# Read-back weight conversions, another order of the PSUM pools and pinned first sevens in an attention + two-MLP kernel

## The chip, the cores and the metric

The kernel runs on one core of a Trainium2 chip. The metric is the device time of one execution in microseconds (us). A core has five engines with queues of their own: TensorE (PE; its weight loads are listed as PEld), VectorE (DVE), ScalarE (ACT), GpSimd (POOL) and SyncE (SP, which here only issues transfers). SBUF is the working memory of 128 partitions, PSUM the eight banks into which PE writes. Every engine takes its own instructions in the order in which they stand in its queue; between engines they wait on semaphores.

## The reference

```python
scores = scale * (q @ k.T); bias = -(cum[:, None] - cum[None, :])      # cum = cumsum(relu(s))
attn = softmax(where(causal, -1e9, scores + minimum(bias, 0)))          # 2 batches, 8 heads, 576 x 576, head size 64
x = (attn @ v) as 1152 tokens x 512
h = x @ w_in; x = maximum(0.01 * h, h) @ w_out                          # 512 -> 2048 -> 512, weights float64
out = sum over 4 experts e of p[:, e] * (maximum(x @ w1[e], 0) @ w2[e]) # 512 -> 1024 -> 512
```

Everything is kept at about fp32 accuracy: a matrix operand is split into a high part (`hi`, rounded to fp32r) and a low part (`lo`, the rest), and a product is three matmuls, hi·hi, lo·hi and hi·lo.

## The kernel before

**Three stages.** In the first, attention runs as 16 *units* (a batch, a pair of heads, the first 256 or the last 320 queries; units 0 to 7 have the first queries, 8 to 15 the last), and the first MLP for the 512 tokens of the first queries (`phases[0]`, functions `opening`, `up1`, `down1`) is woven into it: a matmul group of the MLP between the steps of attention keeps PE busy. When attention ends, what is left of that MLP runs alone: a down block of 48 matmuls, an up piece of 24 and a last down block of 48. In the second stage the first MLP runs for the other 640 tokens, in the third the experts, both with products saved by sums of quarters of the operands (`paired_up`): each weight piece becomes a *seven*, seven sums of quarters of it, hi and lo.

**Attention.** An *item* is one tile of 128 queries of one head. Its steps stand in a pipeline: `scores` (PE writes `ps_sc`, DVE makes `z` and its minimum `mn`), one item later `exps` (ACT on `z`), then `transposes` (PE into `ps_pt`, ACT copies to `pv`), `values` (PE into `ps_o`; at a unit's end DVE normalizes into `xo`), and `finish` (PE transposes `xo` into `ps_x`, ACT copies it to `x`). For units 8 to 15 the keys and queries are split by `split_keys`, one unit ahead: ACT casts `qs`, `ks` and `kd` (`kd` holds the keys once more, beside two rows of `cum` that a transfer brings), POOL makes the low parts of `qs` and `ks`.

**Weights.** `w_in` and `w_out` come as float64. A generator, `supply`, makes them fp32 in 16 *conversions*, each a row of small steps (`converted`): ACT takes the absolute value of the upper words into a `raw` tile, DVE does four operations on it (two `TENSOR_SCALAR`, two `SCALAR_TENSOR_TENSOR`), then `split_w` casts it into a `w` tile (ACT: hi; POOL: lo), and ACT issues a transfer that stores the fp32 values in `w_f32` in HBM, from where the second stage reads them. There are 3 `raw` buffers and 4 `w` buffers (`wpool`). A `w` tile comes free when PE has used it; the split of the fifth conversion and of all later ones so waits for PE, and since ACT takes its queue in order, everything behind the cast waits too. Conversion steps are laid between the attention steps by fixed rules (the loops at lines 707 to 737) and the last ones between the steps of the rest of the MLP (line 746).

**Order.** Up to line 753 every instruction is kept in the order in which it is written (`fixed`, class `InOrder`). Only `fetch`, which loads the weights of the later stages, sets `fixed` to False for itself, and so a scheduler places the loads and sevens of the second stage where it estimates them to fit; from line 753 on the scheduler orders everything.

**PSUM.** While attention runs, the eight banks belong to `ps_mm` (3 banks, MLP), `ps_s` (2, scores), `ps_t` (2, transposes) and `ps_o` (1), in that order. After attention the four pools are closed and `ps_all` takes all eight (line 744). Its tiles go round from the first bank, so its first tile lies where `ps_mm` lay, and may be written only when the tile that was there has been read.

In the profile all instructions go through the recording helper at line 43, so they are told apart by tile names: `raw`, `w` (the sevens' tile is also shown as `w`), `sums` (POOL's sums of quarters), `kd`, `ks`, `qs`, `z`, `pv`, `ht` and `ps_u` (hidden layer), `ps_d` and `y` (down product), `t` (paired tokens), `w_f` (the stored weights).

Of the kernel before, what the change touches and what calls it, by code (L numbers as in the profile page):

```python
# [15 lines left out]
PSUM = bass.MemoryType.PSUM  # L16
# [3 lines left out]
def attention_moe_moe2(ctx: ExitStack, tc: tile.TileContext, q, k, v, s, w_in, w_out, probs, w1, w2, out):  # L20
# [10 lines left out]
    fixed = True  # L31
# [29 lines left out]
    RAW = 3  # L61

# [53 lines left out]
    def converted(n):  # L116

        _, shape, unit = stream[n][:3]
        raw = rawp.tile([P, 1024], F32, tag="raw", name="raw")
        raws.append(raw)  # L120
# [12 lines left out]
        ready.append(split_w(raw, shape, False))  # L133
        nc.scalar.dma_start(w_f32[unit], raw)
        yield

    def supply():

        for n in range(2 * DFF // P // 2):
            yield from converted(n)  # L140
            if len(r64s) < 2 * DFF // P // 2:
                fetch64(len(r64s))
# [10 lines left out]
    def seven(raw):  # L153

        r = raw.rearrange("p (k f) -> p k f", k=KD)
# [5 lines left out]
        nc.gpsimd.tensor_tensor(sums[:, 3], a12, sums[:, 1], ALU.subtract)  # L161
        w = w7pool.tile([P, 2, 7, 2, P], F32R, tag="w7", name="w7", bufs=2)
# [4 lines left out]
        return w  # L167
# [31 lines left out]
    stream, r64s, raws, ready = [], [], [], []  # L199

    def fetch(n):

        nonlocal fixed
        if w7pool is None or len(ready) < 2 * DFF // P // 2:
            return
        was, fixed = fixed, False
        while len(raws) < min(n, len(stream)):
            raws.append(load_w(*stream[len(raws)][:3]))
        while len(ready) < len(raws):
            ready.append(split_w(raws[len(ready)], stream[len(ready)][1], stream[len(ready)][4]))  # L210
        fixed = was

    used, w7pool = 0, None

    def next_w(k):

        nonlocal used
        used += k
        fetch(used + look)
        return ready[used - k : used]  # L220
# [40 lines left out]
    def opening(h):  # L261

        w = next_w(1) + next_w(1)
# [167 lines left out]
    banks = ctx.enter_context(ExitStack())  # L431
    ap = attn.enter_context(tc.tile_pool(name="attn", bufs=2, side="right"))
    ps_mm = banks.enter_context(tc.tile_pool(name="ps_mm", bufs=3, space=PSUM))
    ps_s = banks.enter_context(tc.tile_pool(name="ps_s", bufs=2, space=PSUM))
    ps_t = banks.enter_context(tc.tile_pool(name="ps_t", bufs=2, space=PSUM))
    ps_o = banks.enter_context(tc.tile_pool(name="ps_o", bufs=1, space=PSUM))

# [108 lines left out]
    def split_keys(n):  # L546

        qr, kr = k_raw.pop(n)
# [9 lines left out]
        nc.scalar.copy(kd[:D], kr)  # L558
# [137 lines left out]
    with ExitStack() as phase:  # L696
# [3 lines left out]
        side, units_of_w, opened = attention(), supply(), 0  # L700
        nothing = ps_mm.tile([P, 512], F32, tag="mm", name="nothing")
        with tc.tile_pool(name="early", bufs=1) as early:
# [4 lines left out]
            for at_ in range(3 * 64):  # L707
                i = next(side)
# [10 lines left out]
                if at_ % 3 == 2:  # L719
                    if i in (1, 5):  # L720
                        fetch64(i // 4)
                    if i >= 9 and (i < 19 or i % 2):
                        next(units_of_w)
# [3 lines left out]
        for at_, i in enumerate(side):  # L727
# [5 lines left out]
            else:  # L733
                given += 1.2
# [75 lines left out]
```

## Time and profile before

| what | value |
|---|---|
| runs | 748.47, 749.66, 751.17 us; median 749.66 us |
| the profiled execution | 749.58 us, of which the trace spans 747.8 us |
| PE | busy 718.2 us, 96% of the span, 4388 matmuls |
| DVE, ACT, POOL | busy 418.8, 330.0 and 323.2 us |
| mean granted TensorE clock | 0.990 |
| HBM | 52.58 MB read, 10.82 MB written |

The profile is one execution. The page of slices shows attention in the first 15 or so of 40 slices; from there PE is full to the end. PE's idle time lies before 260 us almost alone. The granted clock is 1.0 (2.4 GHz) but for a few stretches of 0.5 (1.2 GHz): near 54 us, and twice between 220 and 255 us. A time in brackets in a timeline row, `[1.22 <-ACT pv L43]`, is how long the engine sat idle before that row and who ended it.

### The profile page before, as it was taken

The numbers are of one execution on the slowest core, as the hardware profiler recorded it, in microseconds if no ns is written. First come the engines' busy times: TensorE is split into PE (matmuls) and PEld (weight loads), VectorE is DVE, ScalarE is ACT, GpSimd is POOL, SyncE is SP. The second block draws the span as 40 slices with busy tenths as digits, with TensorE's granted clock in tenths as the row PEclk, the third lists the DMA queues.
The fourth block names the chain that finished last, engine by engine and source line by source line (L and its number), as shares of the span: only waits on it lengthen the run. The fifth ranks groups of instructions, "written<-read, shape, count | busy, mean of one in ns | idle before, by whom it ended". The sixth has DMA issues, their size and how long they took to land.

```text
span 747.8 us, 11394 instructions
## 1 busy us (share of the span) xinstructions
PE 718.2 (96%) x4388; PEld 651.2 (87%) x4388; DVE 418.8 (56%) x850; ACT 330.0 (44%) x643; POOL 323.2 (43%) x250
## 2 busy tenths in 40 slices
PE   9889989999998899999999999999999999999998
PEld 8778778888776699999988988989889899898996
DVE  3765686587558545763684443544435445354452
ACT  4677787875653365553351231322314223142220
POOL 4144334443229568894346270542705526143200
PEclk9998999999999999999999999999999999999999
DMA  6794465632432223221011110201102012020002
GB/s 163 203 290 116 135 188 166 179 98 85 167 143 85 58 85 109 88 86 57 30 57 56 57 57 2 85 29 56 57 1 82 33 57 57 0 67 20 1 29 98
DMA packets 39450, 64.14 MB, mean 86 GB/s; under 512 B 3844, under 2 KB 22820, under 8 KB 39396
## 3 DMA queue, kind: packets, MB, share of 16 engines
q1 hardware_dynamic: 30692, 38.26, 17.9%
q10 hardware_dynamic: 8704, 25.17, 9.9%
q8 instruction: 34, 0.56, 0.3%
q14 instruction: 20, 0.16, 0.1%
HBM read 52.58 MB, written 10.82 MB: 85 GB/s over the span
## 4 chain that ended last, share of the span: by engine, by line
PE 83%; DVE 5%; ACT 5%; POOL 3%; issue 3%; ACTq 0%; POOLq 0%; DVEq 0%
PE ps_d L43 38%; PE ps_u L43 32%; PE ps_o L43 5%; PE ps_sc L43 4%; PE ps_pt L43 3%; DVE raw L43 2%; PE nothing L43 2%; POOL w L43 2%; POOL sums L43 1%; ACT w L43 1%; ACT z L43 1%; DVE z L43 1%; ACT raw L43 1%; ACT pv L43 1%; DVE t L43 1%
## 5 line engine op out<-in xcount | busy, mean ns | idle before, releaser
L43 POOL TENSOR_TENSOR w<-raw,w 128x1024 fp32r<-128x1024 f32 (+2 forms) x88 | 147.7, 1694 | 320.7 <-ACT w L43 307.4
L43 PE MATMUL ps_u<-t,w 128*128 128x320 f32 (+1 forms) x1680 | 237.3, 299 | 2.2 <-DVE t L43 1.1
L43 PEld LDWEIGHTS ps_u<-t,w 128*128 128x128 f32 x1680 | 233.2, 189 | 6.3 <-ACT w L43 1.5
L43 PE MATMUL ps_d<-w,ht 128*128 128x512 f32 x864 | 203.3, 391 | 0.0
L43 PEld LDWEIGHTS ps_d<-w,ht 128*128 128x128 f32 x864 | 160.2, 188 | 31.9
L43 ACT ACTIVATE ht<-ps_u 128x320 fp32r<-128x320 f32 (+2 forms) x176 | 74.3, 433 | 158.0 <-DVE ps_u L43 132.0
L43 PE MATMUL ps_d<-ht,w 128*128 128x320 f32 (+1 forms) x576 | 113.5, 346 | 7.8 <-DVE y L43 4.3
L43 ACT CAST w<-raw 128x1024 fp32r<-128x1024 f32 (+2 forms) x88 | 64.0, 758 | 95.8 <-PE ps_d L43 82.0
L43 PEld LDWEIGHTS ps_d<-ht,w 128*128 128x128 f32 x576 | 92.9, 192 | 15.1 <-issue 4.7
L43 DVE SCALAR_TENSOR_TENSOR oacc<-ps_d,pn,oacc 128x512 f32<-128x512 f32 x63 | 47.3, 751 | 104.3 <-PE ps_d L43 104.3
L43 PEld LDWEIGHTS ps_o<-vs,pv 128*128 128x128 f32 x480 | 64.1, 193 | 9.3 <-issue 3.6
L43 DVE TENSOR_TENSOR ps_u<-ps_u,tmp 128x320 f32<-128x320 f32 (+1 forms) x120 | 56.4, 471 | 27.7 <-PE ps_u L43 26.3
L43 DVE SCALAR_TENSOR_TENSOR ht<-ps_u,ht 128x320 fp32r<-128x320 f32 (+1 forms) x128 | 56.3, 452 | 23.3 <-ACT ht L43 22.0
L43 PE MATMUL ps_o<-vs,pv 128*128 128x65 f32 x480 | 63.2, 268 | 3.4 <-DVE xo L43 2.3
L43 POOL TENSOR_TENSOR w<-sums,w 128x1024 fp32r<-128x1024 f32 x24 | 57.9, 2412 | 8.4 <-ACT w L43 8.4
L43 DVE TENSOR_TENSOR tmp<-ps_u,tmp 128x320 f32<-128x320 f32 (+1 forms) x80 | 36.9, 464 | 42.5 <-PE ps_u L43 37.3
L43 PE MATMUL ps_u<-x,w 128*128 128x512 f32 x192 | 58.2, 418 | 0.0
L43 ACT ACTIVATE z<-z,mn 128x256 f32<-128x256 f32 (+4 forms) x80 | 48.6, 607 | 18.6 <-DVE mn L43 16.2
L43 DVE CUSTOM_DVE_ANT_0 z<-ps_sc,mask 128x256 f32<-128x256 f32 (+4 forms) x80 | 40.9, 512 | 26.9 <-PE ps_sc L43 12.4
L43 PE MATMUL ps_pt<-ident,z 128*128 128x128 f32 x240 | 40.9, 279 | 7.5 <-ACT pv L43 7.4
L43 DVE TENSOR_TENSOR ht<-ps_u,ht 128x320 fp32r<-128x320 f32 (+1 forms) x48 | 26.5, 555 | 36.9 <-ACT ps_u L43 36.9
L43 DVE SCALAR_TENSOR_TENSOR raw<-r,raw 128x1024 uint32<-128x1024 uint32 x32 | 45.7, 1429 | 0.2
(72 smaller groups left out, 645.6 us busy)
## 6 DMA issues: line engine op xcount, KB each, us to landing
raw<-in_moe_w_dram SPq DMA_DIRECT2D x32, 512.0 KB, 3.6
r<-in_moe_w_in_dram ACTq DMA_DIRECT2D x8, 1024.0 KB, 7.6
w_f<-raw ACTq DMA_DIRECT2D x16, 512.0 KB, 3.0
r<-in_moe_w_out_dram ACTq DMA_DIRECT2D x8, 1024.0 KB, 5.0
raw<-w_f SPq DMA_DIRECT2D x16, 512.0 KB, 3.4
qr<-in_q_dram SPq DMA_DIRECT2D x16, 160.0 KB, 3.1
kr<-in_k_dram SPq DMA_DIRECT2D x8, 288.0 KB, 7.4
vs<-in_v_dram SPq DMA_DIRECT2D x8, 256.0 KB, 4.2
```

Of the source, the lines that this page charges most:

```text
L43: ins = call(*args, **kw)
```

## The change

- **Store first, split only where a tile is free.** `converted` now issues the store and then splits at once only if unit n's `w` buffer was used by pieces that the MLP has already gone past (`n < retired + WB`, `retired` is set in `next_w`). Otherwise the `raw` tile is given up, and a second generator, `late_splits`, later reads the fp32 values back from HBM (SP's queue) and splits them.
- **Rhythm.** No conversion steps at items 19 to 28; 2.0 steps per item instead of 1.2 at items up to 49, then 1.25. All 16 conversions end before attention does.
- **First sevens pinned.** The two sevens that the second stage starts with are no longer placed by the scheduler; `first_sevens` lays their steps between the MLP's last steps, in written order.
- **PSUM.** `ps_mm` is opened last, so the first five tiles of `ps_all` lie where `ps_s`, `ps_t` and `ps_o` were.
- **`kd` cast on POOL** instead of ACT (8 casts).

```diff
     def converted(n):
@@
-        ready.append(split_w(raw, shape, False))
         nc.scalar.dma_start(w_f32[unit], raw)
+        if n == len(ready) and n < retired + WB:
+            ready.append(split_w(raw, shape, False))
         yield
+    def late_splits():
+
+        while len(ready) < CONVERTED:
+            n = len(ready)
+            if n < min(retired + WB, stored):
+                raw = load_w(*stream[n][:3])
+                yield
+                yield
+                if n == len(ready):
+                    ready.append(split_w(raw, stream[n][1], False))
+            yield
+
     def supply():
-        for n in range(2 * DFF // P // 2):
+        nonlocal stored
+        for n in range(CONVERTED):
             yield from converted(n)
+            stored += 1
@@ the sevens: seven(raw) now runs through seven_steps(raw), which yields between its parts
+    def first_sevens():
+
+        sets_of_seven = []
+        for n in (CONVERTED, CONVERTED + 1):
+            raws[n] = load_w(*stream[n][:3])
+            yield
+            yield
+            for w in seven_steps(raws[n]):
+                if w is not None:
+                    sets_of_seven.append(w)
+                yield
+        while len(ready) < CONVERTED:
+            yield
+        ready.extend(sets_of_seven)
@@
     def next_w(k):
-        nonlocal used
+        nonlocal used, retired
+        retired = used
         used += k
@@
-    ps_mm = banks.enter_context(tc.tile_pool(name="ps_mm", bufs=3, space=PSUM))
     ps_s = banks.enter_context(tc.tile_pool(name="ps_s", bufs=2, space=PSUM))
     ps_t = banks.enter_context(tc.tile_pool(name="ps_t", bufs=2, space=PSUM))
     ps_o = banks.enter_context(tc.tile_pool(name="ps_o", bufs=1, space=PSUM))
+    ps_mm = banks.enter_context(tc.tile_pool(name="ps_mm", bufs=3, space=PSUM))
@@ in split_keys
-        nc.scalar.copy(kd[:D], kr)
+        nc.gpsimd.tensor_copy(kd[:D], kr)
@@ the first loop
-                    if i >= 9 and (i < 19 or i % 2):
+                    if i >= 9 and (i < 19 or i >= 29 and i % 2):
                         next(units_of_w)
@@ the second loop
-                given += 1.2
+                next(late, None)
+                given += 2.0 if i < 50 else 1.25
@@ the rest of the MLP
+        sevens = first_sevens()
         for m, _ in enumerate(main):
+            if m % 2 == 0:
+                next(late, None)
+            if m % 4 == 0:
+                next(tokens, None)
             if m % 4 == 2:
                 next(units_of_w, None)
-            if m % 4 == 0:
-                next(tokens, None)
+            if m % 4 % 2 and m >= 4:
+                next(sevens, None)
```

On PE all 4388 matmuls stand in the same order as before; ACT has 8 casts fewer, POOL 8 more, SP nine more reads of `w_f` (units 7 to 15). What moved is shown at three places. First ACT's queue where unit 8's keys are split, in the middle of the last units of the first kind. Before:

```order
L43 CAST ks<-kr 64x1152
L43 ACTIVATE z<-z,mn 128x128
L43 COPY pv<-ps_pt 128x256
L43 CAST w<-raw 128x1024
L43 DMA w_f_73<-raw 128x1024
L43 CAST kd<-kr 64x1152
L43 ACTIVATE z<-z,mn 128x128
L43 COPY pv<-ps_pt 128x256
```

The same place in the changed kernel:

```order
L43 CAST ks<-kr 64x1152
L43 ACTIVATE z<-z,mn 128x128
L43 COPY pv<-ps_pt 128x256
L43 ACTIVATE z<-z,mn 128x128
L43 COPY pv<-ps_pt 128x256
L43 ACTIVATE z<-z,mn 128x256
```

A conversion's cast and store and the cast of `kd` no longer stand between one item's `pv` copy and the next item's exponential. Second, POOL's queue from the splitting of unit 9's keys on. Before:

```order
L43 TENSOR_TENSOR qs<-qr,qs 64x640
L43 TENSOR_TENSOR ks<-kr,ks 64x1152
L43 TENSOR_TENSOR w<-raw,w 128x1024
L43 TENSOR_TENSOR qs<-qr,qs 64x640
L43 TENSOR_TENSOR ks<-kr,ks 64x1152
L43 TENSOR_TENSOR w<-raw,w 128x1024
```

The same place in the changed kernel:

```order
L43 TENSOR_TENSOR qs<-qr,qs 64x640
L43 TENSOR_TENSOR ks<-kr,ks 64x1152
L43 CAST kd<-kr 64x1152
L43 TENSOR_TENSOR w<-raw,w 128x1024
L43 TENSOR_TENSOR qs<-qr,qs 64x640
L43 TENSOR_TENSOR ks<-kr,ks 64x1152
L43 TENSOR_TENSOR w<-raw,w 128x1024
L43 CAST kd<-kr 64x1152
L43 TENSOR_TENSOR w<-raw,w 128x1024
```

`kd` is now ready only when POOL has come to it, for unit 10 behind the low part of a conversion. Third, ACT's queue where attention ends (`x_98` is the copy of the last `ps_x`; `t_1_...` are the paired tokens; a `w` with a number is a seven). Before:

```order
L43 CAST w<-raw 128x1024
L43 DMA w_f_73<-raw 128x1024
L43 ACTIVATE ht<-ps_u 128x512
L43 ACTIVATE ps_u<-ps_u 128x512
L43 ACTIVATE raw<-r_2367 128x1024
L43 COPY x_98<-ps_x 128x320
L43 CAST t_1_2467<-x_98 128x2x320
L43 CAST w_2573<-raw 128x512
L43 CAST w_2573<-raw 128x256
L43 CAST w_2585<-raw 128x512
L43 CAST w_2585<-raw 128x256
L43 CAST w_2573<-sums 128x1024
```

The same place in the changed kernel:

```order
L43 CAST w<-raw 128x1024
L43 DMA w_f_73<-raw 128x1024
L43 ACTIVATE ht<-ps_u 128x512
L43 ACTIVATE ps_u<-ps_u 128x512
L43 COPY x_98<-ps_x 128x320
L43 CAST w<-raw 128x1024
L43 CAST t_1_2486<-x_98 128x2x320
L43 CAST w_2539<-raw 128x512
L43 CAST t_1_2486<-x_98 128x320
L43 CAST w_2539<-raw 128x256
L43 CAST w_2539<-sums 128x1024
L43 ACTIVATE ht<-ps_u 128x512
```

The last conversion's first step is gone from here, a read-back split stands in its place, and only one seven's casts, not two, stand ahead of the next hidden tile.

## Rows read from the trace of the kernel before

**Rows 1.** Stretches: length; PE, PEld, DVE, ACT, POOL busy (instructions); clock, DMA, GB/s.

```profile
49.00:61.00 12.00, 9.70 (x43) 8.05 (x42) 5.49 (x20) 7.53 (x18) 4.86 (x2) 0.72 0.76 232
61.00:110.00 49.00, 43.89 (x291) 37.81 (x290) 35.04 (x74) 40.92 (x70) 21.37 (x9) 1.00 0.50 151
110.00:215.00 105.00, 100.33 (x659) 88.15 (x657) 70.15 (x135) 74.67 (x124) 37.22 (x16) 1.00 0.45 139
215.00:260.00 45.00, 37.17 (x161) 29.95 (x160) 31.29 (x41) 16.58 (x26) 27.39 (x20) 0.92 0.27 91
```

**Rows 2.** Timeline of PE near 52 us: start, us, instruction, idle before.

```profile
51.92 0.33 PE L43 MATMUL ps_pt<-ident,z 128*128 128x128 f32 x1 [1.22 <-ACT pv L43]
...
54.06 0.69 PE L43 MATMUL ps_pt<-ident,z 128*128 128x128 f32 x2 [0.92 <-ACT pv L43]
```

**Rows 3.** Timeline of ACT near 50 us.

```profile
49.21 1.05 ACT L43 CAST w<-raw 128x1024 fp32r<-128x1024 f32 x1
...
50.16 1.16 ACT L43 CAST kd<-kr 64x1152 fp32r<-64x1152 f32 x1
```

**Rows 4.** Timeline of PE: waits behind a cast of kd, first and last.

```profile
68.08 0.65 PE L43 MATMUL ps_pt<-ident,z 128*128 128x128 f32 x4 [0.97 <-ACT pv L43]
...
164.41 0.66 PE L43 MATMUL ps_pt<-ident,z 128*128 128x128 f32 x4 [0.71 <-ACT pv L43]
```

**Rows 5.** Timeline of ACT near 189 us.

```profile
189.06 1.04 ACT L43 CAST w<-raw 128x1024 fp32r<-128x1024 f32 x1 [5.61 <-PE ps_d L43]
```

**Rows 6.** Timeline of PE near 190 us, first and last of four waits.

```profile
185.20 1.30 PE L43 MATMUL ps_o<-vs,pv 128*128 128x65 f32 x10 [0.76 <-PE ps_pt L43]
...
195.76 0.50 PE L43 MATMUL ps_sc<-ks,qs 128*128 128x512 f32 x1 [0.51 <-DVE mn L43]
```

**Rows 7.** Timeline of PE after attention's last matmul.

```profile
227.08 10.06 PE L43 MATMUL ps_d<-ht,w 128*128 128x512 f32 x36 [4.34 <-DVE y L43]
236.97 5.60 PE L43 MATMUL ps_u<-x,w 128*128 128x512 f32 x24
...
247.63 0.73 PE L43 MATMUL ps_d<-ht,w 128*128 128x512 f32 x2 [3.02 <-ACT ht L43]
248.84 10.01 PE L43 MATMUL ps_d<-ht,w 128*128 128x512 f32 x37 [0.48 <-DVE ht L43]
```

**Rows 8.** Timeline of ACT in the same stretch.

```profile
221.16 1.05 ACT L43 CAST w<-raw 128x1024 fp32r<-128x1024 f32 x1 [5.42 <-DVE raw L43]
...
234.02 1.06 ACT L43 CAST w<-sums 128x1024 fp32r<-128x1024 f32 x1 [4.95 <-POOL sums L43]
```

**Rows 9.** POOL's groups by form, 18 to 250 us: busy us, mean ns.

```profile
L43 POOL TENSOR_TENSOR w<-raw,w 128x1024 fp32r<-128x1024 f32 x16 | 38.1, 2378 | 99.8 <-ACT w L43 86.7 <-PE ps_sc L43 8.2 <-PE ps_o L43 2.5
L43 POOL TENSOR_TENSOR ks<-kr,ks 64x1152 fp32r<-64x1152 f32 x8 | 22.4, 2804 | 7.8 <-ACT ks L43 4.8 <-POOL qs L43 1.6 <-DVE mn L43 1.2
L43 POOL TENSOR_TENSOR sums<-raw 128x256 f32<-128x256 f32 x6 | 6.2, 1049 | 0.2
```

**Rows 10.** Timeline of POOL near 65 us, and of PE near 70 us.

```profile
64.76 3.52 POOL L43 TENSOR_TENSOR ks<-kr,ks 64x1152 fp32r<-64x1152 f32 x1 [0.61 <-POOL qs L43]
...
69.90 0.36 PE L43 MATMUL ps_sc<-kd,qs 66*128 66x448 f32 x1
```

**Rows 11.** Timeline: DVE and POOL near 100 us, PE near 85, DVE near 218.

```profile
100.07 3.39 DVE L43 SCALAR_TENSOR_TENSOR raw<-r,raw 128x1024 uint32<-128x1024 uint32 x1
...
99.72 2.65 POOL L43 TENSOR_TENSOR ks<-kr,ks 64x1152 fp32r<-64x1152 f32 x1 [1.26 <-ACT ks L43]
...
84.69 0.44 PE L43 MATMUL ps_sc<-ks,qs 128*128 128x384 f32 x1 [0.78 <-DVE mn L43]
...
217.82 1.23 DVE L43 SCALAR_TENSOR_TENSOR raw<-r,raw 128x1024 uint32<-128x1024 uint32 x1
```

**Rows 12.** Transfers issued between 60 and 250 us: count, size, median us to landing.

```profile
w_f<-raw ACTq DMA_DIRECT2D x13, 512.0 KB, 2.6
raw<-w_f SPq DMA_DIRECT2D x5, 512.0 KB, 3.5
```

More of the change, by code (lines that the diff above doesn't have):

```diff
@@ L61, in attention_moe_moe2 @@
     RAW = 3
+    WB = 4
+    CONVERTED = 2 * DFF // P // 2
     half = (256, S - 256)
@@ L119, in converted @@
         raw = rawp.tile([P, 1024], F32, tag="raw", name="raw")
-        raws.append(raw)
         r64 = r64s[n]
@@ L132, in converted @@
         yield
-        ready.append(split_w(raw, shape, False))
         nc.scalar.dma_start(w_f32[unit], raw)
+        if n == len(ready) and n < retired + WB:
+            ready.append(split_w(raw, shape, False))
         yield
+    def late_splits():
[8 more added lines that the diff above has]
+            yield
     def supply():
-        for n in range(2 * DFF // P // 2):
+        nonlocal stored
+        for n in range(CONVERTED):
             yield from converted(n)
-            if len(r64s) < 2 * DFF // P // 2:
+            stored += 1
+            if len(r64s) < CONVERTED:
                 fetch64(len(r64s))
@@ L153, in seven, with seven_steps @@
     def seven(raw):
+        steps = seven_steps(raw)
+        while True:
+            w = next(steps)
+            if w is not None:
+                return w
+    def seven_steps(raw):
         r = raw.rearrange("p (k f) -> p k f", k=KD)
@@ L166, in seven @@
             nc.gpsimd.tensor_tensor(lo, of, f32(hi), ALU.subtract)
-        return w
+            if i < 3:
+                yield
+        yield w
+    def first_sevens():
[5 more added lines that the diff above has]
+            for w in seven_steps(raws[n]):
+                if w is not None:
+                    sets_of_seven.append(w)
+                yield
+        while len(ready) < CONVERTED:
+            yield
+        ready.extend(sets_of_seven)
     def split_w(raw, shape, paired):
@@ L197, in in_order @@
                 yield "up", blocks[i], 1
-    stream, r64s, raws, ready = [], [], [], []
+    stream, r64s, raws, ready = [], [], {}, []
+    stored = retired = 0
     def fetch(n):
-        nonlocal fixed
-        if w7pool is None or len(ready) < 2 * DFF // P // 2:
+        if fixed:
             return
[L206 to L211, printed above, removed]
+        for i in range(len(ready), min(n, len(stream))):
+            if i not in raws:
+                raws[i] = load_w(*stream[i][:3])
+        for i in range(len(ready), min(n, len(stream))):
+            ready.append(split_w(raws.pop(i), stream[i][1], stream[i][4]))
     used, w7pool = 0, None
     def next_w(k):
-        nonlocal used
+        nonlocal used, retired
+        retired = used
         used += k
@@ L261, in opening @@
     def opening(h):
-        w = next_w(1) + next_w(1)
+        w = next_w(2)
         ps = [ps_mm.tile([P, 512], F32, tag="mm", name="ps_u") for _ in range(3)]
@@ L699, in attention_moe_moe2 @@
         r64p = phase.enter_context(tc.tile_pool(name="r64p", bufs=2))
-        side, units_of_w, opened = attention(), supply(), 0
+        side, units_of_w, late, opened = attention(), supply(), late_splits(), 0
         nothing = ps_mm.tile([P, 512], F32, tag="mm", name="nothing")
@@ L744, in attention_moe_moe2 @@
         ps_mm = ctx.enter_context(tc.tile_pool(name="ps_all", bufs=8, space=PSUM))
+        sevens = first_sevens()
         for m, _ in enumerate(main):
+            if m % 2 == 0:
+                next(late, None)
+            if m % 4 == 0:
+                next(tokens, None)
             if m % 4 == 2:
                 next(units_of_w, None)
-            if m % 4 == 0:
-                next(tokens, None)
+            if m % 4 % 2 and m >= 4:
+                next(sevens, None)
+        for _ in sevens:
+            pass
         for _ in tokens:
```

## The prediction

> **What bounds the kernel now.** I read the table by stretch first: before 260 us PE stands still in places, and from there on it is full. Since PE executes the same matmuls in the same order before and after, the time is PE's own work plus what PE waits plus what it loses while its clock is low, and only these two can change. Four stretches have nearly all of it [rows 1]: 49 to 61 us (12.00 − 9.70 = 2.3 us idle, and a granted clock of 0.72, which over 12 us is 0.28 × 12 = 3.4 us of full-speed work lost), 61 to 110 us (5.1 us idle), 110 to 215 us (4.7 us) and 215 to 260 us (7.8 us idle, clock 0.92, 0.08 × 45 = 3.6 us). A kernel that saved all of this would take 749.6 − 26.9 = 722.7 us. I set the sum against the profiled execution's 749.6 us, which is 0.1 us under the median of the runs shown, so no correction is needed.
>
> Next, the timelines of PE say who ended each wait. Near 52 us PE waits twice for a `pv` copy, 1.22 and 0.92 us [rows 2], and ACT, which makes that copy, has just done a conversion's cast of 1.05 us and the cast of `kd` of 1.16 us [rows 3]. The half-speed clock begins right behind those two waits. Near 189 us ACT stood 5.61 us before a conversion's cast until PE had freed a `w` buffer [rows 5], and behind it PE itself was short of `pv`, `z` and `mn` four times, 2.5 us in all, of which the first and the last are shown [rows 6]. After attention PE waits 4.34 us for DVE's reading of a `ps_d` bank and 3.02 and 0.48 us for the last hidden tile [rows 7]. In both cases DVE or ACT was late only because its queue held conversion steps and sevens: ACT stood 5.42 us for DVE's last conversion steps and 4.95 us for POOL's sums [rows 8].
>
> **The change part by part.** *49 to 61 us.* ACT loses one cast of 1.05 and one of 1.16 us ahead of the first `pv` copy, 2.2 us, against PE waits of 1.22 + 0.92 = 2.1 us [rows 2, 3]. I take −2.1 us. The next conversion's first step stays where it was, so some of the second wait may live on. The clock fell only behind these two waits and stayed up through the single ones of 61 to 215 us [rows 1, 4], so I take the whole 3.4 us as gained. Term: −5.5 us, between 0 and −5.7.
>
> *61 to 215 us.* Gains: four PE waits of 0.97, 0.79, 1.03 and 0.71 us (the first and last are shown [rows 4]) come right behind a `kd` cast on ACT and go with it, −3.5 us. The ACT wait for a `w` buffer cannot come any more, since a split is written only when PE is past the buffer's last user: −2.5 us [rows 5, 6].
>
> Costs: first, the `kd` cast has no row on POOL. ACT's row for the same shape is 1.16 us [rows 3], POOL's subtraction of the same shape 2.8 us on average [rows 9]; I take 2.6 us, the shortest of these subtractions, as it is the same engine. It stands behind `ks` and sometimes behind a conversion's low part (2.38 us). Unit 9's `ks` was done on POOL at 64.76 + 3.52 = 68.28 us and PE read its `kd` at 69.90 [rows 10]: 68.28 + 2.6 is 1.0 us late. Of the eight units four have so little room (0.2 to 1.6 us by the same reckoning); their sum is 2.4 us. With a cast of 1.16 us it would be under 0.5 us; with one of 5.6 us (twice POOL's row, as when it has to wait for DVE) 15 us. What is queued behind it on POOL is the next conversion's low part, which PE reads items later. Second, between 66 and 100 us two conversions more are squeezed in: 8 DVE operations. In 61 to 215 us 48 such operations stood beside 9.8 us of PE idle time, 0.2 us each, so +1.6 us (0 to 5). Third, nine reads of 3.5 us and their waiting for a `raw` buffer go through SP's queue, ahead of keys and values that are fetched one to two units early: 0. Term: −3.5 − 2.5 + 2.4 + 1.6 = −2.0 us; bounds −8 and +11.
>
> One row speaks against this part. A conversion step on DVE that takes 1.23 us alone took 3.39 us when it met POOL's `ks`, 99.72 to 102.37 us [rows 11]; it ended about one such step after POOL did. The Trainium skill, "SBUF — State Buffer", section "SBUF: two separate sides", says that VectorE operations with two SBUF inputs (or in a two-port mode) and GpSimd operations take a shared port pair as an exclusive lock, and that the loser blocks for the whole instruction. The trace agrees, and by that rule every cast moved to POOL is one more chance to block a DVE step; it is the first rival below.
>
> *215 to 260 us.* With `ps_mm` opened last, the next five tiles go to banks of scores, transposes and outputs, whose last readers are attention's own. No conversion step is left for DVE. So the 4.34 us go: after attention PE does 36 matmuls of the down block at full speed, 36 × 5.60 / 24 = 8.4 us instead of 10.06, and 24 of the up piece, 5.6 us [rows 7], and comes to the last down block at about 222.7 + 8.4 + 5.5 = 236.6 us (times as before, without the earlier gains). What is late then is the split of unit 15. POOL has the sums of the first seven first. Their source is the read-back of unit 16; the last store goes out when DVE ends the last conversion, about 219 us (217.82 + 1.23 [rows 11]), lands 2.6 us later and is read back in 3.5 [rows 12], 225.2 us. Four sums of 1.05 us [rows 9] end at 229.4, the seven's low parts of about 5 us at 234.5. Meanwhile ACT must evict the hidden tile of 233.8 us (1.2 us), cast paired tokens (1.3) and then unit 15 (1.05): 237.4, and POOL's low part of 2.38 us is done at 239.7. PE can do 6 matmuls without it, to 238.0. New wait: 1.7 us, with the 3.02 and 0.48 us gone. The two stretches of half speed followed the waits of 4.34 and 3.02 us, so their 3.6 us go too. Term: −7.8 − 3.6 + 1.7 = −9.7 us. Bounds: −11.4, and −4 if only the bank's wait goes.
>
> The wait for weights near 271 us and all later ones stay, as order and loads are the same there. **Sum:** 749.6 − 5.5 − 2.0 − 9.7 = 732.4 us.
>
> **The rivals.** *POOL and DVE block each other.* Eight casts more on POOL, right behind `ks`, each hold up a DVE step for up to 2.8 us. Behind such a blocked step PE waited 0.78 us at 84.69 us [rows 11]; eight times that is 6.3 us more: 738.7 us. By the Trainium skill's lock this is what the casts would do; without a lock the sum stands. For it: [rows 11]. Against it: DVE works on conversions for less than half of the time, and the lock goes to whoever is first. With casts so long that PE waits for `kd` as well (15 us instead of 2.4), it would be 751.
>
> *The sevens still sit in ACT's queue.* ACT's casts of sums wait for POOL as before, 4.95 us [rows 8], now ahead of two evictions of hidden tiles, and PE meets the same wait of 3.0 + 0.5 us. Then the bank's wait of 4.34 and half the clock loss go, 6.1 instead of 9.7 us: 736.0 us. Against it: the casts of only one seven stand ahead of each eviction.
>
> *Slower: the read-backs block ACT.* Where ACT comes to the cast of a read-back unit before the values have landed, everything behind it in ACT's queue waits, `pv` copies too. Price: 5.61 us on ACT cost PE 2.5 us [rows 5, 6], so a full wait for store and read, 2.6 + 3.5 = 6.1 us [rows 12], costs 2.7. Nine such casts stand in attention's later half and behind it: 24.3 us against a gain of 17.2, 756.7 us; it turns the sign from the seventh full wait on. Against it: a read is issued two items before its cast, some 6 us, and most stores are far back by then; only the last ones are close.
>
> *The waits only change places.* The conversions are all still done, on the same engines and in less time, and PE waits as long as before behind other steps: 749 us. Against it: PE's idle time after attention has its cause in single instructions that are no longer there.
>
> **How the numbers follow.** The forecast has 0.57 (726 to 738 us), the block on POOL 0.14, the sevens 0.14, the read-backs 0.08, changed places 0.07. A measurement of this kernel tells about 0.3%, 2.2 us, from no change. Faster by more: 0.57 + 0.14 + 0.14 less what the first rival has near 751, 0.83; within: 0.08; slower: 0.09. The range goes from 724, where nearly all idle and clock loss is gone, to 744, which takes in the two faster rivals.
>
> **What would show it.** Right: no wait of PE over 1 us for `pv` near 50 us and a clock of 1.0 there; no wait for `y` behind attention, and the second stage's first matmul 9 to 10 us nearer to attention's last; ACT never idle for PE before a cast of `w` during attention. Wrong: PE waits for POOL before `ps_sc<-kd`; DVE steps of 3 us in greater number; ACT idle before casts of `w` for a transfer; a half-speed stretch between 61 and 215 us.

## The result, and the profile after

The changed kernel takes 758.31 us (median; 753.58 to 759.72), the kernel before 749.66 us: ratio 1.0109, 95% interval 1.0084 to 1.0134. It is slower by 8.7 us, where the prediction had it faster by 17. The profiled execution took 758.79 us, of which the trace spans 757.0 us.

PE executes the same 4388 matmuls in the same order in every kernel of this document (but for a few swaps between 273 and 286 us in e14, e15 and e18), so each matmul's start can be set against that of the same matmul before. The table gives what each stretch of the kernel before lost (+) or gained (−) in us, stretch by stretch; the sum is the shift of the last matmul. Each row is one profiled execution.

```
kernel                                   49-61  61-110  110-215  215-260  after    sum
changed kernel                            -4.9   +13.4     +6.1     -5.6    0.0   +9.1
the prediction's terms                    -5.5        -2.0          -9.7    0
```

Two of three terms have the right sign. The middle one, −2.0 us, came out at +19.5 us. The stretches of the changed kernel, with the columns of [rows 1]:

```profile
49.00:61.00 12.00, 10.64 (x69) 8.45 (x67) 9.55 (x31) 9.87 (x24) 7.43 (x4) 1.00 0.86 205
61.00:110.00 49.00, 41.23 (x244) 35.66 (x245) 32.70 (x60) 33.70 (x58) 24.38 (x12) 0.90 0.54 175
110.00:215.00 105.00, 96.12 (x580) 84.15 (x578) 74.48 (x133) 61.65 (x103) 38.59 (x18) 0.92 0.48 159
215.00:260.00 45.00, 41.32 (x217) 34.42 (x216) 32.28 (x40) 24.05 (x40) 24.21 (x14) 0.96 0.38 133
```

Against [rows 1] the clock of the first stretch went from 0.72 to 1.00, as forecast. But in the second and third, where it had been 1.00, it is now 0.90 and 0.92: 0.10 × 49 + 0.08 × 105 = 13.3 us of full-speed work lost. Some two thirds of the 19.5 us are clock, the rest is idle time. Who ended PE's waits between 61 and 215 us (sum in us, count, longest):

```profile
PE ps_o L43 <- issue: 5.1, 3, 2.4
PE ps_pt L43 <- ACT pv L43: 5.0, 5, 1.8
PE ps_sc L43 <- DVE mn L43: 3.7, 4, 2.0
PE ps_o L43 <- DVE xo L43: 3.2, 1, 3.2
PE ps_sc L43 <- POOL kd L43: 0.3, 1, 0.3
```

The same view of the kernel before has these:

```profile
PE ps_pt L43 <- ACT pv L43: 5.0, 7, 1.0
PE ps_sc L43 <- DVE mn L43: 2.7, 4, 1.2
PE ps_x L43 <- ACT pv L43: 1.1, 1, 1.1
PE ps_o L43 <- PE ps_pt L43: 0.8, 1, 0.8
PE ps_o L43 <- issue: 0.2, 1, 0.2
```

The waits of `ps_pt` for `pv` have the same sum as before, those before `ps_o` went from 1.0 to 8.3 us. The longest waits stand before `ps_o`, that is, before the first values of a new unit: PE may write the single `ps_o` bank again only when DVE has read the last unit's sums into `xo`. One such place, near 172 us, engine by engine (DVE, ACT, POOL, PE; start, length, instruction, idle time before it):

```profile
169.16 0.08 DVE L43 DVE_READ_ACCUMULATOR2_ANT mn<- 128x1 f32 x1
172.51 3.81 DVE L43 TENSOR_SCALAR raw<-raw 128x1024 f32<-128x1024 f32 x2 [3.27 <-ACT raw L43]
176.24 0.54 DVE L43 CUSTOM_DVE_ANT_0 z<-ps_sc,mask 128x384 f32<-128x384 f32 x1
...
177.72 0.56 DVE L43 TENSOR_TENSOR xo<-ps_o,st 128x384 f32<-128x384 f32 x1
...
171.32 1.15 ACT L43 ACTIVATE raw<-r 128x1024 f32<-128x1024 f32 x1
...
171.83 2.38 POOL L43 TENSOR_TENSOR w<-raw,w 128x1024 fp32r<-128x1024 f32 x1
174.16 1.61 POOL L43 CAST kd<-kr 64x1152 fp32r<-64x1152 f32 x1
...
178.38 1.94 PE L43 MATMUL ps_o<-vs,pv 128*128 128x65 f32 x8 [2.40 <-issue]
```

DVE stood 3.27 us before a conversion's two TENSOR_SCALARs, because ACT came to the absolute value that they need only at 171.32 us. The two then took 3.81 us, beside two POOL operations, instead of the 1.42 us that the same pair takes further below. The Trainium skill, "SBUF — State Buffer", section "SBUF: two separate sides", says that VectorE operations in a two-port mode and GpSimd operations take a shared port pair as an exclusive lock, and that the other fully blocks; the row agrees if these two run in such a mode, which no row shows. Behind them in DVE's queue stood `z` and `xo`. `xo` ended at 177.72 + 0.56 = 178.28 us, and PE went on at 178.38; the view names "issue", but it is `xo` that came last. An estimate from these rows: with a pair of 1.42 us `xo` would have ended 2.39 us earlier, at 175.89 us, and PE was free only at 178.38 − 2.40 = 175.98 us, so the late start and the slow pair were both needed for this wait. And the clock falls; the stretch from 178 to 186 us, with the columns of [rows 1]:

```profile
178.00:186.00 8.00, 7.62 (x33) 6.93 (x33) 4.70 (x10) 1.20 (x2) 0.00 (x0) 0.57 0.00 0
```

PE is busy there nearly throughout, at little more than half speed.

Behind attention, against [rows 7]:

```profile
239.43 10.04 PE L43 MATMUL ps_d<-ht,w 128*128 128x512 f32 x36 [0.87 <-DVE y L43]
249.31 5.60 PE L43 MATMUL ps_u<-x,w 128*128 128x512 f32 x24
254.75 1.75 PE L43 MATMUL ps_d<-ht,w 128*128 128x512 f32 x7
258.35 3.94 PE L43 MATMUL ps_d<-ht,w 128*128 128x512 f32 x16 [1.84 <-POOL w L43]
```

The wait for `y` went from 4.34 to 0.87 us, the two for `ht` are gone, and the new wait for POOL's `w` is 1.84 us (1.7 forecast). One half-speed stretch is left: 36 matmuls still take 10.04 us.

### The profile page after: what moved, and what is told of

Its sections match the earlier page's. It is cut to its first block, busy times and chain, and to the rows that moved or that the text cites. A ratio compares the mean times of both kernels' runs of the same rounds, so it can differ in the third digit from the quotient of the medians.

```text
span 757.0 us, 11405 instructions
## 1 busy us (share of the span) xinstructions
PE 724.6 (96%) x4388; PEld 656.7 (87%) x4388; DVE 430.8 (57%) x850; ACT 322.9 (43%) x635; POOL 337.3 (45%) x258
## 4 chain that ended last, share of the span: by engine, by line
PE 84%; DVE 7%; ACT 4%; issue 3%; POOL 2%; ACTq 0%; POOLq 0%; DVEq 0%
PE ps_d L43 38%; PE ps_u L43 33%; PE ps_o L43 5%; DVE raw L43 4%; PE ps_sc L43 4%; PE ps_pt L43 3%; ACT raw L43 1%; PE nothing L43 1%; POOL w L43 1%; ACT pv L43 1%; ACT w L43 1%; DVE z L43 1%; DVE t L43 1%; PE ps_x L43 1%; ACT z L43 0%
## 5 line engine op out<-in xcount | busy, mean ns | idle before, releaser
L43 PEld LDWEIGHTS ps_o<-vs,pv 128*128 128x128 f32 x480 | 67.1, 201 | 17.1 <-issue 12.3
L43 PE MATMUL ps_o<-vs,pv 128*128 128x65 f32 x480 | 66.3, 277 | 10.7 <-DVE xo L43 5.5
L43 PE MATMUL ps_u<-x,w 128*128 128x512 f32 x192 | 59.9, 429 | 0.0
L43 DVE SCALAR_TENSOR_TENSOR raw<-r,raw 128x1024 uint32<-128x1024 uint32 x32 | 53.9, 1683 | 0.2
L43 DVE TENSOR_SCALAR raw<-raw 128x1024 f32<-128x1024 f32 (+1 forms) x32 | 35.9, 1121 | 25.7 <-ACT raw L43 25.1
L43 PE MATMUL ps_pt<-ident,z 128*128 128x128 f32 x240 | 42.6, 288 | 6.2 <-ACT pv L43 6.1
```

The source lines that it names most:

```text
L43: ins = call(*args, **kw)
```

## The experiments

Each is timed against the kernel before on the same chip (its medians there were 748.89 to 750.35 us). A pair is named by the two conversion steps that fall in one item: step 1 is ACT's absolute value, 2 DVE's two TENSOR_SCALARs, 3 and 4 its SCALAR_TENSOR_TENSORs, 5 the store and split. Theory A below is that the rhythm of the conversion steps makes the loss; its rivals are the cast of `kd` on POOL and the read-backs.

```
kernel                                   49-61  61-110  110-215  215-260  after    sum
e1  kd on ACT                             -3.8   +14.0     +3.7     -7.2    0.0   +6.9
e2  rhythm of before                      -2.3    +1.5     -1.5     +1.0   +0.3   -0.4
e3  both                                   0.0    +0.4     -1.1     +0.6   +0.3   +0.3
e4  before, PSUM order alone              -2.1    +1.3      0.0     -0.2    0.0   -1.3
e6  no stretch of two steps, pair 4-5     -4.9    +0.5     -2.5     -2.7    0.0   -9.2
e7  pair 5-1, stretch of two stays        -4.9   +10.9     -4.4     -6.3   +0.3   -4.1
e8  even spread, pair 1-2                 -2.8    +8.0     +6.4     -7.9    0.0   +4.1
e9  even spread, pair 5-1                 -2.8    +4.0     -2.2     -1.2    0.0   -1.6
e10 e6, single steps from item 28         -2.5    +2.8     -1.9     -2.1    0.0   -3.3
e11 e6, kd on ACT                         -3.8    +6.1     -2.6      0.0    0.0   -0.4
e12 e10, kd on ACT                        -2.5    +7.8     -1.2     -2.1    0.0   +2.6
e13 e10, PSUM order of before             -1.4    +6.1     +2.4     -3.8    0.0   +3.6
e14 e6, banks changed later               -4.8    +0.5     -2.5     -1.2   -1.2   -8.6
e15 before, banks changed later           -2.1    +1.3      0.0     -4.5   -1.3   -7.1
e16 no stretch of two steps, pair 5-1     -4.8    -0.4     -0.1     -3.2    0.0   -8.3
e17 no stretch of two steps, pair 1-2     -4.8    +3.7     +1.0     +1.6   +0.3   +2.4
e18 e16, banks changed later              -4.8    -1.1     -0.9     -1.1   -1.3   -9.0
```

A caution on single rows: e4 and e15 have −2.1 and +1.3 in the first two stretches with nothing changed there. Differences of some 2 us in a row are not read. A row is one execution and need not be the median: those of e2 and e7 are 2 us and that of e10 is 4 us faster than the kernel's median, those of e1 and e13 are 2 us and that of e11 is 4 us slower.

**e1 to e4: which part.** e1 to e3 undo parts of the changed kernel, e4 does one in the kernel before.

```diff
e1, e3:
-        nc.gpsimd.tensor_copy(kd[:D], kr)
+        nc.scalar.copy(kd[:D], kr)
e2, e3:
-                    if i >= 9 and (i < 19 or i >= 29 and i % 2):
+                    if i >= 9 and (i < 19 or i % 2):
-                given += 2.0 if i < 50 else 1.25
+                given += 1.2
e4, in the kernel before:
-    ps_mm = banks.enter_context(tc.tile_pool(name="ps_mm", bufs=3, space=PSUM))
     ps_s, ps_t, ps_o = ...
+    ps_mm = banks.enter_context(tc.tile_pool(name="ps_mm", bufs=3, space=PSUM))
```

e1. 

> The changed kernel with the kd cast back on ScalarE, nothing else undone. Between 61 and 215 us (counted in the kernel before) the changed kernel lost 19.7 us on the same matmuls. Theory A, the rhythm (two conversion steps per item up to item 49, later 1.25): the cast has little to do with it, 755 to 759 us, and the losses near 80 and 105 us stay. Theory B, the kd casts on GpSimd hold up VectorE's conversion steps and PE: most of the 19.7 us goes, 738 to 744 us. Theory C, the read-backs block ScalarE: 755 to 759 us.

e2. 

> The changed kernel with the rhythm of the conversion steps of before (odd items from 19 on as well, then 1.2 steps per item throughout), kd still on GpSimd, read-backs, bank order and pinned sevens as changed. Theory A: the loss of 13.6 us between 61 and 110 us goes and some of the 6 us after it; the 5 us won near 52 us may go too, since the early conversions stand there again: 741 to 750 us. Theory B: no more than 3 us from the changed kernel, 755 to 760 us. Theory C: as B, for the read-backs stay.

e3. 

> The changed kernel with both undone: kd cast on ScalarE and the rhythm of before. What is left of the change is the store ahead of the split, the read-backs, the bank order and the pinned sevens. If A and B together have the whole loss: 739 to 745 us, the gain of some 5.6 us behind attention and the wait of ScalarE near 189 us gone. Theory C: 750 us or more, with ScalarE idle before casts of read-back tiles for a transfer.

e4. 

> The kernel before with the bank order alone changed (the MLP's pool opened last). If the wait of 4.34 us for y near 227 us came from the first tile of the new pool lying in the MLP's banks, that wait and about half of the 3.6 us of low clock behind it go: 743 to 746 us. If it came from anything else, 749 to 751 us and the wait stays.

Measured: e1 754.69 us (ratio 1.0065, 1.0039 to 1.009), e2 751.49 (1.0017, 0.9998 to 1.0036), e3 749.88 (0.9996, 0.9976 to 1.0017), e4 748.49 (0.999, 0.998 to 0.9999). With the rhythm of before the loss of 61 to 215 us is gone (e2, e3), whether `kd` is cast on POOL or on ACT. So the rhythm makes it. With `kd` back on ACT alone it stays at 17.7 us (e1), but in part as another loss: PE waits 0.97 us for `pv` again, as in [rows 4], and here the clock is low behind it (e1's matmul, and its stretch from 64 to 74 us with the columns of [rows 1]).

```profile
64.45 1.12 PE L43 MATMUL ps_pt<-ident,z 128*128 128x128 f32 x4 [0.97 <-ACT pv L43]
...
64.00:74.00 10.00, 9.55 (x42) 9.33 (x43) 2.73 (x11) 4.84 (x10) 3.04 (x2) 0.51 0.35 112
```

e2 and e3 keep the store and read-backs and lose nothing between 61 and 215 us, so that rival is out too. But both lie above the ranges that I expected (741 to 750 and 739 to 745 us): with the rhythm of before the gain behind attention goes as well (+1.0 and +0.6 us), and PE waits 5.0 and 5.1 us for `y` there. So what e2 and e3 keep of the change, store first, read-backs, bank order and pinned sevens, gains nothing that shows; of these only the bank order was tried by itself. And e4 does not gain behind attention: the order of the banks is not what the wait for `y` hangs on. In e4 it is as long as in [rows 7]:

```profile
225.93 10.03 PE L43 MATMUL ps_d<-ht,w 128*128 128x512 f32 x36 [4.34 <-DVE y L43]
```

**e6 to e9: which part of the rhythm.** At 1.25 steps per item every fourth item has two, and as a conversion has five steps, they are always the same two. In the changed kernel, from item 50 on, they are 1 and 2: ACT's absolute value, and directly behind it DVE's operations that read it. The start of the count chooses the pair.

```diff
e6:                              (pair 4-5 from item 39 on)
-                given += 2.0 if i < 50 else 1.25
+                given += 1.25
e7:                              (pair 5-1 from item 50 on)
-        owed = given = 0
+        owed, given = 0, 0.25
e8, e9: e6's line, the first loop as before, and given = 0.75 (e8: pair 1-2) or -0.25 (e9: pair 5-1)
```

e6. 

> The changed kernel without the stretch of two conversion steps per item (items 39 to 49 get 1.25 as the later ones). At 1.25 every fourth item gets two steps, and since a conversion has five, it is the same two each time: here its last two, the second SCALAR_TENSOR_TENSOR on DVE and the store (in the changed kernel from item 50 on its first two, ACT's absolute value and DVE's TENSOR_SCALARs). One conversion less is done by attention's end. Theory 'two per item' (the stretch of two steps alone does it, and what is lost later is its consequence): the loss of 61 to 110 us (13 us against the kernel before at the same matmul) goes, and that of 110 to 215 us (8 us) goes too; the gains at 49 to 61 and behind attention stay in part: 741 to 746 us. Theory 'which pair' (two steps of one conversion in one item, for which the second waits on another engine): the loss of 61 to 110 us gets smaller, but 5 to 10 us stay over 61 to 215 us, as DVE's last step and the store that waits for it lie in one item: 748 to 754 us.

e7. 

> The changed kernel with the count of owed steps started at 0.25 instead of 0: the stretch of two steps per item stays as it is, and from item 50 on the two steps that fall in one item are the store of one conversion and the absolute value of the next, both on ACT, instead of absolute value and TENSOR_SCALARs. Amount and rate of the work are the same. Theory 'which pair': the 8 us that the changed kernel loses between 110 and 215 us shrink to 0 to 3, the 9 us before 110 us stay: 750 to 754 us. Theory 'two per item' or 'amount': no difference from the changed kernel, 756 to 760 us.

e8. 

> The changed kernel with the first loop's conversion steps as before (odd items from 19 on too) and 1.25 steps per item all through: conversions are spread evenly and end with attention. Pair: absolute value and TENSOR_SCALARs, as in the changed kernel from item 50 on. Theory 'which pair': against the kernel with the rhythm of before (1.2, where the pair moves on from conversion to conversion; 751.5 us) it loses 4 to 8 us between 61 and 215 us and gains 3 to 5 us behind attention, where no conversion is left: 750 to 755 us. Theory 'two per item': no loss in 61 to 215 us, the gain behind attention: 745 to 748 us.

e9. 

> As the even spread before it, with the pair store and next absolute value. Theory 'which pair': no loss between 61 and 215 us, the gain behind attention of 3 to 5 us: 745 to 748 us, some 5 us under the other pair. Theory 'two per item': the same time as the other pair, 745 to 748 us both. If the gain behind attention has nothing to do with conversion steps left over there: 750 to 752 us.

Measured: e6 741.05 us (0.99, 0.9871 to 0.9928), e7 747.64 (0.997, 0.9955 to 0.9985), e8 752.94 (1.0042, 1.0019 to 1.0065), e9 747.9 (0.9975, 0.9956 to 0.9993). One number, the start of the count, is worth 10.7 us in the changed kernel (e7) and 5.0 us with an even spread (e9 against e8), at the same amount of work. e9 came out where I expected it, but not for the reason given: the gain behind attention is 1.2 us, not 3 to 5, and PE waits 6.33 us for `y` there. In e7 the loss of 110 to 215 us turned into a gain of 4.4, more than I expected, and that of 61 to 110 stayed. Its stretch from 110 to 215 us, and then DVE, ACT and PE at the place shown above:

```profile
110.00:215.00 105.00, 102.46 (x660) 91.32 (x661) 72.20 (x148) 71.99 (x121) 42.08 (x18) 0.97 0.55 179
```

```profile
164.05 1.42 DVE L43 TENSOR_SCALAR raw<-raw 128x1024 f32<-128x1024 f32 x2
...
169.86 0.56 DVE L43 TENSOR_TENSOR xo<-ps_o,st 128x384 f32<-128x384 f32 x1
...
162.85 1.13 ACT L43 ACTIVATE raw<-r 128x1024 f32<-128x1024 f32 x1 [0.30 <-ACT pv L43]
...
170.56 1.25 PE L43 MATMUL ps_o<-vs,pv 128*128 128x65 f32 x10
```

ACT's step now lies an item ahead, the TENSOR_SCALARs begin without a wait, `xo` is ready at 170.42 us, and PE does not wait.

e6, without the two steps per item of items 39 to 49, has neither loss, and it is the fastest of these four. Here "two per item" was right (741 to 746 us) and "which pair" expected too much loss (748 to 754): with pair 4-5 it is ACT that waits for DVE's last step, 22.9 us in 10 waits between 49 and 265 us, and no loss shows in these two stretches:

```profile
61.00:110.00 49.00, 45.02 (x292) 38.17 (x293) 32.77 (x70) 35.23 (x64) 22.63 (x11) 1.00 0.52 155
110.00:215.00 105.00, 101.96 (x666) 89.99 (x665) 69.55 (x138) 72.34 (x122) 46.18 (x21) 1.00 0.47 153
```

So both parts of the rhythm cost: the stretch of two steps 10.4 us (e7 against e6 in 61 to 110 us), pair 1-2 10.5 us (changed kernel against e7 in 110 to 215 us). In the medians the stretch costs 6.6 us (e7 against e6), since e7 gains more behind attention. e8 and e9 lose 4 to 8 us in 61 to 110, near one `xo` that a DVE step of 2.52 us holds up; that step ran beside POOL's `ks` (DVE, POOL, PE of e9):

```profile
63.80 2.52 DVE L43 SCALAR_TENSOR_TENSOR raw<-r,raw 128x1024 uint32<-128x1024 uint32 x1
...
67.11 0.42 DVE L43 TENSOR_TENSOR xo<-ps_o,st 128x256 f32<-128x256 f32 x1
...
62.59 2.64 POOL L43 TENSOR_TENSOR ks<-kr,ks 64x1152 fp32r<-64x1152 f32 x1 [1.35 <-issue]
...
67.63 1.71 PE L43 MATMUL ps_o<-vs,pv 128*128 128x65 f32 x10 [1.37 <-issue]
```

From 70 to 80 us the clock of e9 is 0.57, against 1.00 in e2, which has the same wait at the same place (the first line is e9's, the others are e2's):

```profile
70.00:80.00 10.00, 10.00 (x46) 9.35 (x45) 3.72 (x12) 5.22 (x9) 1.70 (x2) 0.57 0.23 63
...
68.06 1.30 PE L43 MATMUL ps_o<-vs,pv 128*128 128x65 f32 x10 [1.38 <-issue]
...
70.00:80.00 10.00, 10.00 (x70) 9.05 (x69) 5.04 (x15) 8.65 (x15) 3.38 (x2) 1.00 0.47 147
```

So the same wait costs 1.4 us in e2 and 0.43 × 10 = 4.3 us of full-speed work more in e9; what decides it, these runs do not show.

**e10 to e13: the last conversion, `kd`, and the banks once more.**

```diff
e10, e12, e13: e6, and
-                    if i >= 9 and (i < 19 or i >= 29 and i % 2):
+                    if i >= 9 and (i < 19 or i >= 28):
e11, e12: kd on ACT, as in e1
e13: ps_mm opened first, as before
```

e10. 

> The even kernel without the stretch of two steps (741.05 us; pair: last STT and store) with a conversion step at every item from 28 on instead of at odd items from 29: five steps more, so that the last conversion ends with attention and not behind it. Theory 'leftover steps' (the wait for y behind attention, 3.8 us, and the half-speed stretch there come from DVE's conversion steps that stand among the last MLP's sums): the wait goes to under 1 us, 3 to 6 us are gained behind attention, and 0 to 2 us lost at 50 to 75 us, where the five steps now lie: 736 to 740 us. If the wait for y is the bank's: 741 to 743 us, with the wait as it was.

e11. 

> The kernel without the stretch of two steps (741.05 us), with kd cast on ACT again. If the cast on POOL costs by POOL's and DVE's mutual blocking (DVE's slow steps of 2.5 us and more) as it seemed in the changed kernel (3.6 us): 738 to 740 us. If the cast on ACT costs what I forecast (3.5 us of waits for pv, and the clock near 52 us): 743 to 747 us, with pv waits behind kd and a half-speed stretch near 52 us.

e12. 

> Single steps from item 28 on and kd on ACT together. If both effects add: 733 to 738 us if kd on POOL costs, 739 to 744 us if kd on ACT costs.

e13. 

> Single steps from item 28 on, kd on POOL, and the PSUM pools in the order of before (ps_mm first). Theory 'bank order' of the forecast: the wait for y of about 4 us behind attention comes back, with a half-speed stretch: 4 to 7 us more than the kernel with single steps alone. Theory 'leftover steps': no difference over 1 us.

Measured: e10 750.11 us (1.0004, 0.999 to 1.0017), e11 745.02 (0.9958, 0.9935 to 0.9981), e12 752.35 (1.0043, 1.0027 to 1.0059), e13 751.62 (1.003, 1.0019 to 1.0042). e10 missed: the five steps moved forward bring back a loss at 61 to 110 us (2.8 us in e10's row, 6.1 in e13's), and the last two STTs now end attention, directly ahead of `y`, so that wait is 4.46 us instead of 3.81. e11 says that here `kd` on POOL is the better place, by 4.0 us, the opposite of e1 in the changed kernel, where ACT was better by 3.6. e12 against e10 points the same way, by 2.2 us. So the sign depends on the rhythm around it. e11's twelve executions lie in two groups, seven at 742.0 to 745.2 us with a mean clock of 0.992 to 0.997 and five at 749.3 to 749.8 with 0.986 to 0.988: the same program has more or less half speed from one execution to the next. Against the lower group's median, 743.88 us, `kd` on POOL gains 2.8 us. e13 has the wait for `y` at 3.81 us, and gains no less than e10 behind attention (3.8 and 2.1 us): the bank order changes nothing there. In the medians it is 1.5 us slower, more than the 1 us I allowed and well short of the 4 to 7 us of "bank order".

**e14 to e18: the change of banks, the third pair, and both together.**

```diff
e14 (in e6), e15 (in the kernel before), e18 (in e16):
-        banks.close()
-        ps_mm = ctx.enter_context(tc.tile_pool(name="ps_all", bufs=8, space=PSUM))
         for m, _ in enumerate(main):
             ...
+    banks.close()
+    ps_mm = ctx.enter_context(tc.tile_pool(name="ps_all", bufs=8, space=PSUM))
     fixed = False
e16, e17: e6 with given started at 1.0 (pair 5-1) or 2.0 (pair 1-2)
```

e14. 

> The kernel without the stretch of two steps (741.05 us), with the pools of attention closed and the eight banks opened only behind the rest of the MLP, which so goes on in its three banks. If the wait for y (3.8 us) comes from changing pools, all old tiles having to be read first: it goes, and 3 to 6 us with the half-speed stretch behind it, if nothing else is late: 735 to 739 us. If it comes from DVE being behind with its sums, which PE needs whatever the pools: it stays, 740 to 743 us.

e15. 

> The kernel before with the same edit alone. If the change of pools makes the wait for y of 4.34 us: it goes, 743 to 747 us. If not: 748 to 751 us.

e16. 

> The kernel without the stretch of two steps, its count of owed steps started at 1.0: one step earlier throughout, and the two steps in one item are store and next absolute value, both on ACT. Theory 'which pair': as the pair of last STT and store, 739 to 744 us, no half-speed stretch between 110 and 215 us. Rival 'any shift costs': 746 us or more.

e17. 

> The same, started at 2.0: two steps earlier throughout, and the two in one item are absolute value (ACT) and TENSOR_SCALARs (DVE, which wait for it). Theory 'which pair': 6 to 10 us slower than the other two, 747 to 752 us, with DVE waiting for ACT's raw and half-speed stretches between 140 and 190 us. If the pair does not matter by itself: 740 to 744 us.

e18. 

> Both remedies together: no stretch of two steps, pair store and next absolute value, pools of attention closed behind the rest of the MLP. If they add: the wait for y of 2.2 us and a half-speed stretch of 3.4 us go, 736 to 739 us. If the wait for the last hidden tile (2.4 us) or the last unit's split grows by what is gained, as with the other pair: 740 to 743 us.

Measured: e14 741.85 us (0.9884, 0.9868 to 0.9901), e15 742.12 (0.9896, 0.987 to 0.9923), e16 741.37 (0.9878, 0.9854 to 0.9902), e17 751.26 (1.0012, 0.9998 to 1.0026), e18 740.68 (0.9887, 0.9871 to 0.9904).

e6, e16 and e17 differ in the start of the count alone, and so in the pair and by one or two steps in how far the conversions are: 741.05, 741.37 and 751.26 us. The start that gives pair 1-2 costs 10 us; e17 against e16 it is 4.1, 1.1 and 4.8 us in the last three stretches up to 260 us, so half of it lies where attention ends and behind it. DVE's waits for ACT's absolute value between 61 and 215 us, in e16 and in e17:

```profile
DVE raw L43 <- ACT raw L43: 6.2, 7, 1.4
```

```profile
DVE raw L43 <- ACT raw L43: 21.2, 10, 4.0
```

In the changed kernel this is 19.7 us in 10 waits, in e6 0.9. My expectation put e17's half-speed stretches between 140 and 190 us; they are not there (its clock is 1.00 from 110 to 215 us). Up to 215 us it loses in small waits, those for `mn` (4.8 us in 7) the largest, more of it before 110 us (+3.7) than behind (+1.0), and behind attention PE waits 5.8 us for `y`, with conversion steps left over there.

e15 takes 8 us off the kernel before by moving two lines, a little more than I expected (743 to 747 us). PE goes straight through the place of the wait for `y`, at full speed:

```profile
220.50 9.12 PE L43 MATMUL ps_d<-ht,w 128*128 128x512 f32 x39
229.94 3.02 PE L43 MATMUL ps_u<-x,w 128*128 128x512 f32 x12 [0.32 <-DVE y L43]
...
241.71 10.32 PE L43 MATMUL ps_d<-ht,w 128*128 128x512 f32 x37 [2.08 <-DVE ht L43]
```

So that wait comes with the change from one set of pools to the other, whatever their order. In e4, by the order of the pools, the first new tile lies where `ps_s` lay, and PE still waits for `y`, which reads a bank of `ps_mm`: the first tile of the new pool waits for readers of the old ones, and not only for that of its own bank. In e14 the same edit gains as much at that place, and gives it back: PE then waits for the last unit's split.

```profile
236.65 0.79 PE L43 MATMUL ps_d<-ht,w 128*128 128x512 f32 x1 [3.46 <-ACT w L43]
239.40 11.02 PE L43 MATMUL ps_d<-ht,w 128*128 128x512 f32 x41 [1.96 <-POOL w L43]
```

e18 shows the same: 0.7 us under e16, with 2.4 us of waiting for `ht` in the place of the 2.2 us for `y`. In both, what comes next behind attention is late too. e6, e14, e16 and e18 all beat both kernels, by 17 us against the changed one and by 8 to 9 us against the kernel before; they are not told apart.

## Why the prediction was wrong, point by point

**49 to 61 us: right.** −5.5 forecast, −4.9 measured, clock 1.00, and of the waits for `pv` there are 0.42 and 0.75 us left. e11 with `kd` on ACT keeps −3.8 and e2 with the old steps −2.3; the two parts are not cleanly told apart, since −2.1 came in e4 without either.

**61 to 215 us: wrong, and this is the step that failed:** the price of the conversion steps laid closer. The prediction said: "between 66 and 100 us two conversions more are squeezed in: 8 DVE operations. [...] 0.2 us each, so +1.6 us". That is a mean over steps of which nearly all lay one to an item (by the trace over 42 of them, not 48, which makes it +1.9 us). Measured: the stretch of two steps costs some 10 us, and the 1.25 steps per item behind it, for which the sum has no term at all, another 10, because that rate locks the pair 1-2. Two things were missing. The price of a step on DVE is not its length but what stands directly behind it: once in six items that is `xo`, for which PE has no other bank. And I counted no clock here, since it "stayed up through the single ones of 61 to 215 us" [rows 1, 4]; those were of 0.7 to 1.2 us. The longest waits that came were of 1.2 to 3.2 us, and the clock made 13.3 of the 19.5 us. That it stayed up in the kernel before was luck: in e1 it is low behind a wait of 0.97 us. The row of 0.78 us [rows 11] held the warning, PE waiting for an `mn` that stood behind a slow conversion step on DVE, and I used it for the wrong rival.

The smaller terms of that stretch: the ACT wait for a `w` buffer [rows 5, 6] is gone, as forecast; the changed kernel gains some 2.3 us near 190 us (shift +17.0 to +14.7). `kd` on POOL takes 1584 ns, not my 2.6 us, and PE waited for it 0.3 us in all, not 2.4:

```profile
L43 POOL CAST kd<-kr 64x1152 fp32r<-64x1152 f32 x8 | 12.7, 1584 | 0.3
```

The waits behind `kd` on ACT went, but 5.0 us of waits for `pv` stand elsewhere. In e6, without the packed steps, the whole stretch came out at −2.0 us, the sum that I had forecast, but by luck: its waits for `pv` there are 4.8 us, hardly less than the 5.0 us before, where the sum has −3.5.

**215 to 260 us: the sign right, the reason wrong.** −9.7 forecast, −5.6 measured. "With `ps_mm` opened last [...] the 4.34 us go" fell with e4 and e13. The sentence behind it, "No conversion step is left for DVE", is the reason that held: the wait is 0.9 us in the changed kernel, e1 and e7, where no conversion step stands between `xo` and `y`. With steps left over it is 2.2 to 6.3 us (e2, e3, e6, e9, e16, e17), and with the last two ending attention 3.8 to 4.5 us, in either order of the banks (e10, e13). The chain from the hidden tile over paired tokens and split to a new wait of 1.7 us held: 1.84. One of two half-speed stretches stayed.

**The rivals.** Slower came true, but not by the read-backs: ACT waited for a transfer once, 0.7 us. Steps slowed beside POOL are real, 3.81 us for a pair of 1.42, but the casts of `kd` do not make the loss: e2 keeps them on POOL and has none, and they cost 3.6 us by e1 and gain 4.0 us by e11. Nor does the slowing in sum: between 61 and 215 us DVE is busy 65.2 us with conversion steps in the changed kernel and 68.2 us in e16, which is 17 us faster. The sevens' rival fell, as both waits for `ht` are gone. Of the signs of being wrong the half-speed stretches between 61 and 215 us came true.

## What to carry to other kernels

When filler work is laid between the steps of a pipeline, look at where each piece falls, not at how many there are: a rate that divides the pieces evenly repeats one pattern for ever, and where a producer and its consumer on two in-order engines fall in one slot, the engine that PE hangs on should not be the one that waits. ACT waited 22.9 us for DVE in e6 and no loss showed, while DVE's 19.7 us for ACT came with a loss of 10. Before crediting a wait to a buffer, move the buffer alone; here two lines on the point at which pools are changed did what the reordering did not.

## What the runs showed of the hardware that was not expected

- Behind a wait of PE the granted clock can be low for longer than the wait: 0.57 from 178 to 186 us behind 2.40 us, 0.57 from 70 to 80 us in e9 behind 1.37 us, 0.51 from 64 to 74 us in e1 behind 0.97 us (1.0 is TensorE's 2.4 GHz, 0.5 its 1.2 GHz). The length of the wait does not decide it: behind 0.97 us in the kernel before [rows 4] and 1.38 us in e2 the clock is 1.00. The same program has more or less of it from one execution to the next (e11).
- A cast of 64x1152 from fp32 to fp32r takes 1.58 us on POOL, 1.16 us on ACT [rows 3], and 2.8 us as POOL's subtraction with two inputs [rows 9].
